# Raw weights fetched ahead, the first decay rows straight from SBUF: a change to the opening of a fused attention and two-MLP kernel

## The chip, the cores and the metric

The kernel runs on one core of a Trainium2 chip. The metric is the device time of one execution in microseconds (us); lower is better. Before the change it is 960.9 us, the median of 3 runs (960.6 to 962.42).

## What is computed

Three blocks follow one another: a causal attention with a decay, a layer that takes the maximum of three products, and a layer with a rational gate.

```python
scores = scale * np.matmul(q, k.transpose(0, 1, 3, 2))      # batch 4, 8 heads, 576 rows, width 64
cum = np.cumsum(np.log(np.clip(f, 0.0001, 1.0)), axis=-1)
scores = np.where(causal, -1e9, scores + cum[..., :, None] - cum[..., None, :])
attn = softmax(scores);  x = attn @ v                       # 2304 tokens of 512
h = np.maximum(np.maximum(x @ w1, x @ w2), x @ w3)          # 768 wide
x = h @ w_out
h = x @ w_in                                                # 2048 wide
out = (P(h) / (Q(h) + 1e-6)) @ w_out2
```

The weights arrive as 64-bit floats. They are fetched as pairs of 32-bit words, and the kernel itself makes 32-bit floats of them.

## The kernel before, in words

**Attention.** Work goes by pairs of heads; a pair holds two units, one for each head, for one group of query rows (320 or 256 of the 576). The first four pairs are those of the first batch with the group of 320. For a pair, `load` fetches the keys `kn` and queries `qn`, `load_v` the values; `prepare` transposes keys and queries on TensorE (tiles `tk`, `tq`), copies them into `kf` and `qf`, and in `copies` fetches two rows of the decay into `kf`. A unit then makes scores in three blocks of 64, 192 and 320 keys (`s`, L378), reduces them on VectorE (L382), takes exponentials on ScalarE (L388), normalises on GpSimd (L397), transposes back on TensorE (`tp`, L417), and, once both heads of a pair are there, multiplies by the values (`o`, L433). VectorE writes the result into `x` (L441). The lines are those of the kernel before.

**The decay.** `ncum` is the running sum of the logarithms, one scan over 576 columns for all 32 rows; `nch` holds it as a rounded part and a remainder. `nch` goes to `ncd` in DRAM, and every `kf` is filled from `ncd`.

**Fillers.** `exercised` puts `WARM` = 2 matmuls of 128x512 on a constant tile (`<-warm`, L84) ahead of the real work in each PSUM tile of the first four pairs. They compute nothing that is used.

**Weights.** Each of the 18 pieces of w1, w2, w3 goes through a conversion: `load_raw` (L165, 512 KB), a magnitude on ScalarE (`cv_w`, L179), four integer operations on VectorE (L184, L185, L186, L189), the rounded part on ScalarE (L195) and the remainder on GpSimd (L198). 12 smaller pieces of w_out follow. `pipelined` issues loads two conversions ahead (`LOOK`), and `conv_due` says at each fill how many conversions should be left.

**Order.** All loads are issued by SyncE (SP). Apart from the last stage, a scheduler with a model of time sets the order on each engine; `keep_in_program_order` holds single instructions in the order of the code. Each engine then runs its list strictly in order. The first product of the second block (`h`, L465) needs `x` of all four first pairs. From 74.45 us on TensorE works on that block between the units, and from 560 us on, at the latest, on the third block.

Of the kernel before, what the change touches and what calls it, by code (L numbers as in the profile page):

```python
# [8 lines left out]
F32 = mybir.dt.float32  # L9
F32R = mybir.dt.float32r  # L10
I32 = mybir.dt.int32
AF = mybir.ActivationFunctionType
ALU = mybir.AluOpType
# [11 lines left out]
GQ = [(0, 320), (320, 576)]  # L25
# [12 lines left out]
def kernel(  # L38
    ctx: ExitStack, tc: tile.TileContext, q, k, v, f, w1, w2, w3, w_out, m2_in, m2_out, m2_a, m2_b, out
):  # L40
    nc = tc.nc
    B, H, S, D = q.shape
# [3 lines left out]
    P = 128  # L46
# [6 lines left out]
    def r32(ap):  # L53
        return ap.bitcast(F32)

    def move(dst, src):
        return nc.sync.dma_start(r32(dst), r32(src))
# [7 lines left out]
    apool = apool_cm.enter_context(tc.tile_pool(name="apool", bufs=1, side="right"))  # L65
# [9 lines left out]
    warm = mpool.tile([P, 4, P], F32R, name="warm", tag="xo", bufs=2)  # L75
    for i in range(4):
        nc.vector.tensor_copy(warm[:, i], ident)
    wide = warm.rearrange("p i c -> p (i c)")

    def exercised(bank, n):  # L80

        if n < 4:
            for _ in range(WARM):
                nc.tensor.matmul(bank, warm[:, 0], wide, start=True, stop=True)  # L84
        return bank

    WARM = 2
# [13 lines left out]
    NR = B * H  # L101
    fl = apool.tile([NR, S], F32, name="fl", tag="vs", bufs=3)
    nc.sync.dma_start(fl, f.rearrange("b h s -> (b h) s"))
    ones = apool.tile([NR, S], F32, name="ones", tag="e4_0")
    nc.vector.memset(ones, 1.0)
    nc.vector.tensor_scalar(fl, fl, 1.0e-4, 1.0, op0=ALU.max, op1=ALU.min)
    nc.scalar.activation(fl, fl, AF.Ln)
    ncum = apool.tile([NR, S], F32, name="ncum", tag="vs", bufs=3)
    nc.vector.tensor_tensor_scan(ncum, ones, fl, 0.0, op0=ALU.mult, op1=ALU.subtract)
    nch = apool.tile([NR, 2, S], F32R, name="nch", tag="pt0")  # L110
    nc.vector.tensor_copy(nch[:, 0], ncum)
    nc.vector.tensor_tensor(nch[:, 1], ncum, r32(nch[:, 0]), op=ALU.subtract)
    ncd = dram.tile([NR, 2, S], F32R, name="ncd")
    move(ncd, nch)


    NKB, NQB = 4, (2, 3)
# [2 lines left out]
    LOOK, WHOLE, PRE = 2, 6, 2  # L120
# [123 lines left out]

        return [a, b, h, last]

    def pipelined(work, look):

        n = len(work)

        def go(i):
            for j in range(0 if i == 0 else i + look, min(i + look + 1, n)):
                work[j][0]()
            work[i][1]()

        return [lambda i=i: go(i) for i in range(n)]
# [5 lines left out]
    def pinned(ld):  # L262
        tc.keep_in_program_order(ld)
# [12 lines left out]
    class Pair:  # L276
# [58 lines left out]
        def copies(self):  # L335
            khi = GQ[self.groups[-1]][1]
            for h, i in enumerate(self.ik):
                k2 = kfs[i] if self.whole else k_split(i)[1]
                pinned(move(k2[D : D + 2, :khi], ncd[self.b * H + 2 * self.hp + h][:, :khi]))

        def prepare(self):
            return (
# [157 lines left out]
    def moe1_units(b, g):  # L500
        return [lambda fc=fc, j=j: moe1_h(b, g, fc, j) for fc in range(NF1) for j in range(3)] + [
            lambda dc=dc: moe1_o(b, g, dc) for dc in range(NDC)
        ]
# [14 lines left out]
        for fc in range(NF1)  # L518
        for z in range(2)
    ]  # L520
    conv = pipelined(conv, LOOK)
    wps = [(c, z) for c in range(NF2) for z in range(2)]
    conv2 = []
    for i, cz in enumerate(wps):
# [38 lines left out]
            state["of"] = max(1, NFILL * (ends[at] - step) - 3)  # L563
            state["n"], state["m"] = len(units), 0

    NCONV = len(conv)
    state["c"] = state["c2"] = 0.0

    def conv_due(step):
# [1 line left out]
        return NCONV - int(state["c"])  # L571

    pairs[0].load()
    pairs[0].load_v()
    LV = 1
    lvat = {}
    for p in pairs[1:]:
        lvat.setdefault(max(0, first[p.n] - LV), []).append(p)
    for f_ in pairs[0].prepare():
        f_()  # L580
    pairs[1].load()
    ab = const.tile([P, 8], F32, name="ab")
    pinned(nc.sync.dma_start(ab[:, 0:4], m2_a.partition_broadcast(P)))
    pinned(nc.sync.dma_start(ab[:, 4:6], m2_b.partition_broadcast(P)))
    for step in range(len(slots) + 2):
        u = slots[step] if step < len(slots) else None
        t = slots[step - 1] if 0 <= step - 1 < len(slots) else None
# [8 lines left out]
        if o:  # L596
            o.attend()
            if step in ready:
                queue.append((step, [x for bg in ready[step] for x in moe1_units(*bg)]))
        fill(step)  # L600
        if t:
            t.turn(0)
# [238 lines left out]
```

## Time and profile before

| what | value |
|---|---|
| median of 3 runs | 960.9 us |
| the profiled execution | 960.97 us |
| its span, first to last instruction | 959.2 us |
| TensorE busy | 935.4 us (98%) |
| VectorE busy | 729.2 us (76%) |
| ScalarE busy | 640.5 us (67%) |
| GpSimd busy | 253.6 us (26%) |
| granted TensorE clock, mean | 0.991 of full |

The profiled execution lies 0.07 us above the median, and 1.8 us of it lie outside the span. Busy time of TensorE counts the fillers too, so 98% isn't 98% of needed work. PE is TensorE's matmuls, DVE is VectorE, ACT ScalarE, POOL GpSimd; SPq is SyncE's list of transfers.

### The profile page before, as it was taken

Reading aid. Unit: us, or ns where it says so; the run is one execution under the profiler, and the core shown is the slowest. Engines: PE = TensorE matmul, PEld = TensorE weight load, DVE = VectorE, ACT = ScalarE, POOL = GpSimd, SP = SyncE. Lnnn points to the kernel's source line nnn. Section 1 sums busy time; section 2 is a strip of 40 time slices with the busy share of each in tenths; the row PEclk is TensorE's granted clock in tenths of the full one; section 3 lists DMA queues with packets and bytes.
Section 4 is the critical chain, followed back from the end, with each engine's and each line's share of the span. In section 5 each row is a group of like instructions: output and inputs, shape, how many; then the busy total and the mean of one; then the engine's idle time right before and its main releaser. Section 6 shows DMA issues by size and latency. Waiting matters only on the chain.

```text
span 959.2 us, 16834 instructions
## 1 busy us (share of the span) xinstructions
PE 935.4 (98%) x5780; PEld 827.2 (86%) x5780; DVE 729.2 (76%) x1689; ACT 640.5 (67%) x1526; POOL 253.6 (26%) x408
## 2 busy tenths in 40 slices
PE   8989899999999999999999999999999999999998
PEld 6758889997998989999999988888888888899997
DVE  5698985556676776634296969888988988899997
ACT  6886667777777676656444567667666666677765
POOL 2546654444554555424132400000000000000000
PEclk9978999999999999999999999999999999999999
DMA  6694323123456455220145477011002102100000
GB/s 164 167 247 138 84 68 85 43 76 86 131 152 193 139 168 145 86 90 1 58 139 179 144 252 275 1 44 44 1 1 66 44 1 66 45 1 1 33 1 33
DMA packets 125621, 88.52 MB, mean 92 GB/s; under 512 B 74448, under 2 KB 110304, under 8 KB 125536
## 3 DMA queue, kind: packets, MB, share of 16 engines
q1 hardware_dynamic: 125536, 87.45, 30.4%
q8 instruction: 46, 0.75, 0.3%
q14 instruction: 39, 0.32, 0.1%
HBM read 64.73 MB, written 22.69 MB: 91 GB/s over the span
## 4 chain that ended last, share of the span: by engine, by line
PE 76%; DVE 13%; ACT 4%; issue 3%; DMA 2%; SPq 1%; POOL 1%; ACTq 0%; POOLq 0%; DVEq 0%
PE hq L716 7%; PE hq L714 7%; PE oo L764 7%; PE oo L765 7%; PE hq L715 7%; PE oo L763 7%; PE h L465 5%; PE h L466 5%; PE h L467 5%; PE o L433 5%; PE tp L417 4%; PE s L380 2%; PE s L381 2%; PE x2p L491 2%; PE x2p L493 1%
## 5 line engine op out<-in xcount | busy, mean ns | idle before, releaser
L465 PE MATMUL h<-x,w1h 128*128 128x320 f32 (+1 forms) x576 | 176.2, 306 | 2.0 <-DVE x L441 1.1
L466 PE MATMUL h<-x,w1h 128*128 128x320 f32 (+1 forms) x576 | 172.7, 300 | 0.0
L467 PE MATMUL h<-x,w1l 128*128 128x320 f32 (+1 forms) x576 | 172.5, 300 | 0.0
L397 POOL TENSOR_SCALAR e<-e,rs 128x64 f32<-128x64 f32 (+4 forms) x160 | 88.8, 569 | 105.0 <-DVE rs L394 96.4
L388 ACT ACTIVATE e<-e,st 128x64 f32<-128x64 f32 (+4 forms) x160 | 89.1, 558 | 37.7 <-DVE st L382 36.7
L465 PEld LDWEIGHTS h<-x,w1h 128*128 128x128 f32 x576 | 109.9, 191 | 4.9 <-DVE x L441 2.0
L764 PE MATMUL oo<-wp,gh 128*128 128x512 f32 x288 | 112.6, 391 | 0.0
L763 PE MATMUL oo<-wp,gh 128*128 128x512 f32 x288 | 112.0, 389 | 0.0
L466 PEld LDWEIGHTS h<-x,w1h 128*128 128x128 f32 x576 | 110.0, 191 | 0.3 <-issue 0.2
L467 PEld LDWEIGHTS h<-x,w1l 128*128 128x128 f32 x576 | 109.9, 191 | 0.1
L723 ACT ACTIVATE s<-hq 128x512 f32<-128x512 f32 (+1 forms) x80 | 44.3, 554 | 98.0 <-PE hq L716 98.0
L765 PE MATMUL oo<-wp,gl 128*128 128x512 f32 x288 | 109.1, 391 | 0.0
L382 DVE CUSTOM_DVE_ANT_0 e<-s,mask 128x320 f32<-128x320 f32 (+3 forms) x160 | 67.8, 432 | 38.2 <-PE s L381 22.9
L419 ACT ACTIVATE pt<-tp 128x384 f32<-128x384 f32 (+3 forms) x160 | 69.8, 468 | 16.6 <-PE tp L417 13.8
L726 DVE SCALAR_TENSOR_TENSOR s<-s,ab,u 128x512 f32<-128x512 f32 (+1 forms) x80 | 55.7, 696 | 32.6 <-ACT u L724 32.4
L417 PE MATMUL tp<-ident,e 128*128 128x128 f32 (+1 forms) x480 | 77.4, 279 | 3.0 <-DVE k2s L310 1.7
L716 PE MATMUL hq<-x,wil 128*128 128x512 f32 (+1 forms) x192 | 69.8, 364 | 0.0
L714 PE MATMUL hq<-x,wih 128*128 128x512 f32 (+1 forms) x192 | 69.8, 363 | 0.0
L715 PE MATMUL hq<-x,wih 128*128 128x512 f32 (+1 forms) x192 | 69.6, 363 | 0.0
L765 PEld LDWEIGHTS oo<-wp,gl 128*128 128x128 f32 x288 | 54.0, 188 | 11.2
L763 PEld LDWEIGHTS oo<-wp,gh 128*128 128x128 f32 x288 | 54.1, 188 | 10.5
L764 PEld LDWEIGHTS oo<-wp,gh 128*128 128x128 f32 x288 | 54.0, 188 | 10.5
(131 smaller groups left out, 2429.4 us busy)
## 6 DMA issues: line engine op xcount, KB each, us to landing
raw_w<-in_moe_w_dram SPq DMA_DIRECT2D x18, 512.0 KB
raw_wp<-in_moe_w_out_dram SPq DMA_DIRECT2D x32, 256.0 KB
wpd<-wp SPq DMA_DIRECT2D x32, 256.0 KB
raw_wi<-in_moe_w_in_dram SPq DMA_DIRECT2D x32, 256.0 KB
wp<-wpd SPq DMA_DIRECT2D x10, 768.0 KB
x2d<-xo SPq DMA_DIRECT2D x16, 320.0 KB
out_dram<-ob SPq DMA_DIRECT2D x18, 256.0 KB
kn<-in_k_dram SPq DMA_DIRECT2D x32, 128.0 KB
```

What stands on the lines that cost most here:

```text
L388: nc.scalar.activation(e[:nr], e[:nr], AF.Exp, bias=m, scale=-1.0, accum_out=l)
L397: nc.gpsimd.tensor_scalar(e, e, self.rs[:, 1, j : j + 1], 0.0, op0=ALU.mult, op1=ALU.add)
L417: nc.tensor.transpose(tp[:kr, dst : dst + P], self.e[i][:, Q0[c] : Q1[c]], ident)
L465: nc.tensor.matmul(hp_[:, :w], wh[:, j, dc], xs[dc][:, 1], start=(dc == NDC - 1), stop=False)
L466: nc.tensor.matmul(hp_[:, :w], wh[:, j, dc], xs[dc][:, 0], start=False, stop=False)
L467: nc.tensor.matmul(hp_[:, :w], wl[:, j, dc], xs[dc][:, 0], start=False, stop=(dc == 0))
L714: nc.tensor.matmul(hp_[:, :w], wih[:, dc, fs], xh, start=(dc == 0), stop=False)
L715: nc.tensor.matmul(hp_[:, :w], wih[:, dc, fs], xl, start=False, stop=False)
L716: nc.tensor.matmul(hp_[:, :w], wil[:, dc, fs], xh, start=False, stop=(dc == NDC - 1))
L763: nc.tensor.matmul(o, g[0][:, ts_], wh_, start=(fc == 0), stop=False)
L764: nc.tensor.matmul(o, g[0][:, ts_], wl_, start=False, stop=False)
L765: nc.tensor.matmul(o, g[1][:, ts_], wh_, start=False, stop=(fc == NF2 - 1))
```

## The change

The scan runs in two stretches (320 and 256 columns), each split into its two parts at once. For the first pair the decay rows go from `nch` in SBUF straight into `kf`, a row at a time, in place of the way over `ncd`. The first three raw weights are fetched right behind the first pair's keys and queries; the first pair's values and the write of `ncd` come behind its `prepare`. Two conversions are put into the code ahead of the second pair's loads, with `NCONV` lowered by two, so that all later ones keep the same distance. The fillers of the first pair are held in program order. The two tiny loads of the third block's coefficients (`ab`) go to step 16.

```diff
             for _ in range(WARM):
-                nc.tensor.matmul(bank, warm[:, 0], wide, start=True, stop=True)
+                dense = nc.tensor.matmul(bank, warm[:, 0], wide, start=True, stop=True)
+                if n == 0:
+                    tc.keep_in_program_order(dense)
...
-    nc.vector.tensor_tensor_scan(ncum, ones, fl, 0.0, op0=ALU.mult, op1=ALU.subtract)
-    nch = apool.tile([NR, 2, S], F32R, name="nch", tag="pt0")
-    nc.vector.tensor_copy(nch[:, 0], ncum)
-    nc.vector.tensor_tensor(nch[:, 1], ncum, r32(nch[:, 0]), op=ALU.subtract)
+    for a, z in GQ:
+        part = slice(a, z)
+        sofar = ncum[:, a - 1 : a] if a else 0.0
+        nc.vector.tensor_tensor_scan(ncum[:, part], ones[:, part], fl[:, part], sofar, op0=ALU.mult, op1=ALU.subtract)
+        nc.vector.tensor_copy(nch[:, 0, part], ncum[:, part])
+        nc.vector.tensor_tensor(nch[:, 1, part], ncum[:, part], r32(nch[:, 0, part]), op=ALU.subtract)
     ncd = dram.tile([NR, 2, S], F32R, name="ncd")
-    move(ncd, nch)
...
-                pinned(move(k2[D : D + 2, :khi], ncd[self.b * H + 2 * self.hp + h][:, :khi]))
+                row = self.b * H + 2 * self.hp + h
+                if self.n == 0:
+                    for x in range(2):
+                        pinned(move(k2[D + x : D + x + 1, :khi], nch[row : row + 1, x, :khi]))
+                else:
+                    pinned(move(k2[D : D + 2, :khi], ncd[row][:, :khi]))
...
-    conv = pipelined(conv, LOOK)
+    ahead = [load_ for load_, _ in conv[: LOOK + 1]]
+    conv = pipelined(conv, LOOK, True)
...
-    NCONV = len(conv)
+    NCONV = len(conv) - 2
...
     pairs[0].load()
-    pairs[0].load_v()
+    for load_ in ahead:
+        load_()
...
     for f_ in pairs[0].prepare():
         f_()
+    move(ncd, nch)
+    pairs[0].load_v()
+    for _ in range(2):
+        conv.pop(0)()
     pairs[1].load()
     ab = const.tile([P, 8], F32, name="ab")
-    pinned(nc.sync.dma_start(ab[:, 0:4], m2_a.partition_broadcast(P)))
-    pinned(nc.sync.dma_start(ab[:, 4:6], m2_b.partition_broadcast(P)))
```

In the lists below the number at a name's end is a running one; the second `kn` and the second `tk` are the second pair's. Line numbers of the changed kernel are higher: L165 is L169 there, L267 and L270 are L271 and L274, L332 is L336, L378 is L387, L417 is L426.

SP's list of transfers before, from the end of the first pair's queries on:

```order
L267 DMA v_140<-in_v_dram 128x2x64
L270 DMA v_140<-in_v_dram 128x2x64 x2
L267 DMA v_285<-in_v_dram 128x2x64
L267 DMA kn_163<-in_k_dram 128x2x64
L57 DMA ncd<-nch 32x1152
L270 DMA kn_163<-in_k_dram 128x2x64 x2
L270 DMA v_285<-in_v_dram 128x2x64
L57 DMA kf_114<-ncd 2x320
L57 DMA kf_115<-ncd 2x320
```

The same place of SP's list in the changed kernel:

```order
L169 DMA raw_w_0_142<-in_moe_w_dram 128x4x256
L169 DMA raw_w_0_144<-in_moe_w_dram 128x4x256
L169 DMA raw_w_0_146<-in_moe_w_dram 128x4x256
L57 DMA kf_116<-nch 1x16x20 x2
L57 DMA kf_117<-nch 1x16x20 x2
L57 DMA ncd<-nch 32x1152
L271 DMA v_169<-in_v_dram 128x2x64
L274 DMA v_169<-in_v_dram 128x2x64 x2
L169 DMA raw_w_1_183<-in_moe_w_dram 128x4x256
L271 DMA kn_194<-in_k_dram 128x2x64
L274 DMA kn_194<-in_k_dram 128x2x64 x2
```

Three raw weights now stand ahead of the first pair's decay rows, and a fourth ahead of the second pair's keys, which stood fourth in the piece before and now stand behind twelve other transfers.

TensorE's list before, from the first pair's first filler on (`s_0_0_0_0` are the scores of its first head, `tp_0_0_0` that head's transposes):

```order
L84 MATMUL s_0_0_0_0_186<-warm 128x512 x2
L84 MATMUL s_0_0_0_0_193<-warm 128x512 x2
L84 MATMUL o_1_0_367<-warm 128x512 x2
L332 MATMUL tq_0_154<-ident,qn_132 128x128 x3
L84 MATMUL tq_0_206<-warm 128x512 x2
L332 MATMUL tk_0_173<-ident,kn_163 128x128 x3
L378 MATMUL s_0_0_0_0_186<-kf_114,qf_118 128x64
L378 MATMUL s_0_0_0_0_193<-kf_114,qf_118 128x192
L84 MATMUL tp_0_0_0_243<-warm 128x512 x2
L84 MATMUL s_0_0_0_0_200<-warm 128x512 x2
L378 MATMUL s_0_0_0_0_200<-kf_114,qf_118 128x320
```

And in the changed kernel, from the second pair's transposes on:

```order
L336 MATMUL tk_0_202<-ident,kn_194 128x128 x3
L84 MATMUL s_0_0_0_0_215<-warm 128x512 x2
L387 MATMUL s_0_0_0_0_215<-kf_116,qf_120 128x64
L84 MATMUL s_0_0_0_0_222<-warm 128x512 x2
L387 MATMUL s_0_0_0_0_222<-kf_116,qf_120 128x192
L336 MATMUL tq_0_235<-ident,qn_193 128x128 x3
L84 MATMUL tp_0_0_0_266<-warm 128x512 x2
L84 MATMUL s_0_0_0_0_229<-warm 128x512 x2
L387 MATMUL s_0_0_0_0_229<-kf_116,qf_120 128x320
L426 MATMUL tp_0_0_0_266<-ident,e_0_0_0_221 128x128
L426 MATMUL tp_0_0_0_266<-ident,e_0_0_0_228 128x128 x2
```

The second pair's transposes of its keys stand ahead of the first scores in both. The fillers of `s` and `o`, six matmuls, moved from ahead of the first transposes of queries to behind them, and the first head's transposes `tp` now stand ahead of the second head's scores, which before ran first.

## Rows read from the trace of the kernel before

**Rows 1.** The page, busy time, share of the span and instructions.

```profile
PE 935.4 (98%) x5780; PEld 827.2 (86%) x5780; DVE 729.2 (76%) x1689; ACT 640.5 (67%) x1526; POOL 253.6 (26%) x408
```

**Rows 2.** Stretches: us, busy PE PEld DVE ACT POOL, clock, DMA share, GB/s.

```profile
10.52:27.84 17.32, 17.14 (x97) 13.39 (x98) 9.26 (x37) 14.59 (x46) 7.53 (x11) 1.00 0.71 188
27.84:50.20 22.36, 22.36 (x133) 17.48 (x132) 13.99 (x46) 18.60 (x57) 11.00 (x18) 1.00 0.63 167
50.20:73.90 23.70, 19.94 (x80) 11.97 (x78) 23.48 (x49) 19.16 (x47) 11.73 (x13) 0.75 0.89 246
79.30:133.76 54.46, 51.33 (x363) 46.26 (x361) 49.52 (x113) 34.09 (x86) 33.03 (x40) 1.00 0.33 88
133.76:142.00 8.24, 6.24 (x39) 5.02 (x39) 5.64 (x16) 6.00 (x17) 6.84 (x11) 1.00 0.19 60
```

**Rows 3.** The line of time, TensorE: start, us, instruction, idle before.

```profile
4.23 1.22 PE L84 MATMUL tk<-warm 128*128 128x512 f32 x2 [4.23 <-DVE warm L77]
...
7.60 1.11 PE L84 MATMUL s<-warm 128*128 128x512 f32 x4
...
9.81 0.71 PE L332 MATMUL tk<-ident,kn 128*128 128x128 f32 x3
10.52 0.79 PE L378 MATMUL s<-kf,qf 66*128 66x64 f32 x4
...
12.08 0.70 PE L378 MATMUL s<-kf,qf 66*128 66x320 f32 x2
...
25.57 1.41 PE L433 MATMUL o<-pt,v 128*64 128x320 f32 x12
```

**Rows 4.** The line of time, SP's issues of transfers.

```profile
4.21 0.47 SPq L267 DMA_DIRECT2D v<-in_v_dram  x1
...
6.31 0.41 SPq L267 DMA_DIRECT2D kn<-in_k_dram  x1
7.02 0.33 SPq L57 DMA_DIRECT2D ncd<-nch  x1
...
9.12 0.59 SPq L57 DMA_DIRECT2D kf<-ncd  x2
...
15.95 1.57 SPq L165 DMA_DIRECT2D raw_w<-in_moe_w_dram  x3
```

**Rows 5.** Waits of SP's list, first 50 us: total, times, longest.

```profile
SPq L270 <- DMA raw_w<-in_moe_w_dram: 1.9, 2, 1.0
SPq L267 <- DMA raw_w<-in_moe_w_dram: 1.3, 1, 1.3
```

**Rows 6.** The line of time, ScalarE.

```profile
11.35 0.35 ACT L388 ACTIVATE e<-e,st 128x64 f32<-128x64 f32 x1
...
19.86 0.67 ACT L179 ACTIVATE cv_w<-raw_w 128x512 f32<-128x512 f32 x1 [0.18 <-DMA raw_w<-in_moe_w_dram]
...
21.43 0.68 ACT L179 ACTIVATE cv_w<-raw_w 128x512 f32<-128x512 f32 x1 [0.35 <-DMA raw_w<-in_moe_w_dram]
```

**Rows 7.** The line of time, VectorE, the decay's scan and remainder.

```profile
4.38 1.35 DVE L109 TENSOR_TENSOR_SCAN ncum<-ones,fl 32x576 f32<-32x576 f32 x1 [0.21 <-ACT fl L107]
...
6.24 0.75 DVE L112 TENSOR_TENSOR nch<-ncum,nch 32x576 fp32r<-32x576 f32 x1
```

**Rows 8.** The line of time, GpSimd, the first unit's normalisation.

```profile
14.73 1.22 POOL L397 TENSOR_SCALAR e<-e,rs 128x64 f32<-128x64 f32 x3 [4.91 <-DVE rs L394]
```

**Rows 9.** VectorE busy on tile cv_w alone, by stretch, with clock and DMA.

```profile
27.84:50.20 22.36, 8.77 (x16) 1.00 0.63 167
50.20:73.90 23.70, 18.67 (x24) 0.75 0.89 246
```

**Rows 10.** TensorE by stretch: us, busy, clock, DMA share, GB/s.

```profile
62.24:74.45 12.21, 9.64 (x29) 0.50 0.62 172
74.45:79.30 4.85, 4.85 (x18) 0.50 0.66 218
```

**Rows 11.** The fillers (L84) alone: us, busy PE and PEld, clock, DMA.

```profile
10.52:74.45 63.93, 31.25 (x90) 14.76 (x90) 0.90 0.74 201
```

More of the change, by code (lines that the diff above doesn't have):

```diff
@@ L105 @@
     nc.vector.memset(ones, 1.0)
+    ncum = apool.tile([NR, S], F32, name="ncum", tag="vs", bufs=3)
+    nch = apool.tile([NR, 2, S], F32R, name="nch", tag="pt0")
     nc.vector.tensor_scalar(fl, fl, 1.0e-4, 1.0, op0=ALU.max, op1=ALU.min)
     nc.scalar.activation(fl, fl, AF.Ln)
-    ncum = apool.tile([NR, S], F32, name="ncum", tag="vs", bufs=3)
-    nc.vector.tensor_tensor_scan(ncum, ones, fl, 0.0, op0=ALU.mult, op1=ALU.subtract)
-    nch = apool.tile([NR, 2, S], F32R, name="nch", tag="pt0")
-    nc.vector.tensor_copy(nch[:, 0], ncum)
-    nc.vector.tensor_tensor(nch[:, 1], ncum, r32(nch[:, 0]), op=ALU.subtract)
+    for a, z in GQ:
[4 more added lines that the diff above has]
+        nc.vector.tensor_tensor(nch[:, 1, part], ncum[:, part], r32(nch[:, 0, part]), op=ALU.subtract)
     ncd = dram.tile([NR, 2, S], F32R, name="ncd")
-    move(ncd, nch)
     NKB, NQB = 4, (2, 3)
@@ L245, in stages_wp, with pipelined @@
         return [a, b, h, last]
-    def pipelined(work, look):
+    def pipelined(work, look, begun=False):
         n = len(work)
         def go(i):
-            for j in range(0 if i == 0 else i + look, min(i + look + 1, n)):
+            for j in range(0 if i == 0 and not begun else i + look + (i == 0), min(i + look + 1, n)):
                 work[j][0]()
@@ L599 @@
                 queue.append((step, [x for bg in ready[step] for x in moe1_units(*bg)]))
+        if step == 16:
+            pinned(nc.sync.dma_start(ab[:, 0:4], m2_a.partition_broadcast(P)))
+            pinned(nc.sync.dma_start(ab[:, 4:6], m2_b.partition_broadcast(P)))
         fill(step)
```

## The prediction

> **What bounds the kernel now.** The page's busy row comes first: TensorE is at work in 935.4 of 959.2 us [rows 1], so 24 us of its idle time, and what its clock loses, are all that can be won. The stretches say where these lie. From 10.52 to 50.20 us TensorE is busy in 39.5 of 39.7 us at the full clock, while VectorE is busy in 9.26 and 13.99 us only [rows 2]. It is busy because of the fillers: they alone take 31.25 us between 10.52 and 74.45 us [rows 11]. An engine that runs its list in order and has no gap there catches nothing up, so whatever delays the first scores at 10.52 us delays the first four pairs by as much. From 50.20 to 73.90 us the bound is VectorE (23.48 of 23.70 us), and 18.67 us of that are 24 operations on `cv_w`, six conversions at 3.11 us. Earlier, 16 operations took 8.77 us, 2.19 us a conversion [rows 2, 9]. TensorE's clock is at half, 1.2 GHz, from 62.24 to 79.30 us [rows 10]. VectorE stays near its limit until 133.76 us (49.52 of 54.46), and TensorE loses 3.13 us in that stretch and 2.00 us in the next one [rows 2].
>
> **The change part by part.** *Decay.* Before, the chain is scan, cast, remainder from 4.38 to 6.99 us [rows 7], then `ncd` is written at 7.02 and `kf` filled from it at 9.12 us [rows 4]. For 320 of 576 columns the first stretch's three operations are 320/576 of 2.61 us, 1.45 us; the second scan, which stands ahead of the first remainder, adds 256/576 of 1.35, 0.60 us. The rows are ready at 6.4 us in place of 7.0, and the way over DRAM, 2.1 us, is gone: `kf` could be asked for 2.7 us sooner.
>
> *Raw weights.* They take from that. Three of them go out where the values' loads went, from 4.21 us on, and the decay rows come behind them in the same list. Before, three raw weights were issued within 1.57 us from 15.95 on [rows 4]; the first one's conversion began at 19.86, the second's at 21.43 us, each right after waiting for its transfer [rows 6]. So one lands 3.9 us after its issue and the next ones 1.57 us apart: they pass one after another. By this the three land at 8.1, 9.7 and 11.3 us, and the decay rows behind them not before 11.3. The Trainium skill's page "DMA: Bandwidth & Descriptors", section "Two DMAs through the same engine are not ordered", says that within one queue of a DMA engine descriptors start in order; the spacing of 1.57 us agrees, and by the page too the small transfer gets no way past the large ones.
>
> *The second pair's keys.* In the list TensorE must transpose them ahead of the first scores, before and after. Before they were issued from 6.31 us on and transposed at 9.81 us [rows 3, 4]. Now the write of `ncd`, three loads of values and a fourth raw weight stand ahead of them. Loads of values and of keys, which read nothing of the weights, already wait for raw weights to land, 1.9 and 1.3 us [rows 5]: SP issues no transfer until the eighth ahead of it is done (the program gives its transfers eight semaphores in turn). Counting back by eight, the three loads of values wait for the three raw weights (8.1, 9.7, 11.3 us), the fourth raw weight and the keys for the decay rows. So that weight goes out at 11.4 and lands at 15.3 us, and the keys, issued from 11.9 to 13.4 us and passing behind it, are there at about 16.0 us. Three transposes (0.71 us) and two fillers (half of 1.11 us) later the first scores start, at 17.2 in place of 10.52 us: **+6.7 us** [rows 3]. Bounds: if SP did not wait, keys issued at 10.4 us and behind the fourth weight would be there at 13.4, +4.2 us; if the fourth weight takes the 4.9 us that the second of the three did from its issue, +7.7 us.
>
> *Conversions.* In VectorE's list four of them now stand ahead of the first reduction: 4 x 2.19 = 8.8 us, which from 8.8 us on end at 17.6 us, about when the first scores are there. They hide behind the wait above and cost nothing more; without it they would hold the first exponential, at 11.35 us before [rows 6], until then. Up to the third `x` there are eight conversions in the list in place of six, between the first and the fourth `x` as many as before. So the stretches from 27.84 to 73.90 us keep their lengths, and two conversions fewer are left behind, 2 x 3.11 = 6.2 us of VectorE [rows 9].
>
> *The order on TensorE.* The first head's `tp` now stands ahead of the second head's scores. From the end of the last scores, 12.78 us, to the end of the normalisation, 15.95 us, it was 3.2 us [rows 3, 8]; TensorE has a pair of fillers to put into that (0.55 us) and waits for the rest, **+2.5 us** (bounds 1.5, if two of the three normalised blocks are enough to go on, and 3.2). The six moved fillers took 1.4 us of a time before the first scores; one pair is in the sum above, the others, **+0.9 us**, now come behind (bounds 0 and 1.4).
>
> *The rest.* The `ab` loads go to a stretch in which transfers are scarce (DMA share 0.33 and 0.19 from 79.30 us on [rows 2]), hidden, and their removal from SP's early list saves nothing, since SP waits for landings there. Holding the fillers in order changes nothing by itself beyond the places shown.
>
> *Sum.* The first product of values, at 25.57 us before [rows 3], comes 6.7 + 2.5 + 0.9 = 10.1 us later, and so do the stretches up to the fourth `x`. Given back is what TensorE loses from 79.30 to 142 us, 5.1 us at most, since VectorE has 6.2 us less to do there; I take 4, as part of these gaps waits for other engines. 10.1 - 4 = +6.1 us. Against the profiled execution's 960.97 us, which is 0.07 us above the median of the runs, that makes **967.0 us**.
>
> **The rivals.**
> *VectorE decides, and the early work is free: faster.* VectorE's work up to 133.76 us is the same in both kernels, and in the first 50 us it sat idle for 8.1 + 8.4 us between 10.52 and 50.20 alone [rows 2]. If the second pair's keys came as early as before and the fillers left gaps to catch up, the two conversions' 6.2 us would be won less some delay: 960.97 - 6.2 + 1 to 4, about 957 us. It decides where the front's delay is below what is given back, 5 us. Against it stand the 39.5 busy us of 39.7 on TensorE. Chance 0.18.
> *Front and give-back cancel.* A delay of 5 us (the lower bound of the keys and a short bubble) and 5.1 us back: 961 us, within 0.2% (1.9 us), which is about what a measurement of this kernel can tell from no change. Chance 0.10.
> *The clock falls in the new wait: slower still.* TensorE would be idle from about 9 to 16 us. In rows 10 the clock was at half after gaps that VectorE had made, and came back 4.85 us after dense work began at 74.45 us; at the start two fillers took 1.22 us against half of 1.11 us later [rows 3]. If it falls, the first 5 us or more of work behind the wait run at half speed: 2.5 us, and with the bubble in between 5 us more. With little given back, 967 + 5 to 8, about 973 us. The Trainium skill's page "TensorE: Matmul & The Clock Gate", section "What's actually happening", says that the throttled state is the default and activity releases it; the trace agrees with a clock that falls at 62.24 us. Chance 0.17.
> *My forecast*, a delay of 9 to 13 us of which 3 to 5 come back: 964 to 971 us. Chance 0.55.
>
> **How the numbers follow.** Slower by over 0.2%: 0.55 + 0.17 = 0.72; same 0.10; faster 0.18. The forecast's own range is 964 to 971 us. For 8 in 10 the range takes in the upper half of the faster case, no change, and most of the fallen clock: 958.5 to 974 us. The lists also differ in places up to some 360 us, where the model of time shifts things; I put that at 2 us either way, the size of the gap in the last stretch of rows 2, an estimate that lies inside.
>
> **What would show it.** In the changed kernel's trace: the decay rows' and keys' transfers waiting for raw weights in SP's list, the first scores at 17 us and the first product of values at 35 to 36 us; a gap on TensorE of some 7 us before the second pair's transposes and one of 2.5 us before the second head's scores; the first `h` at about 84 us, with 14 conversions done, not 12; less idle time of TensorE between then and the eighth unit pair. It is wrong if first scores come before 13 us, or if TensorE shows gaps among the fillers that take the delay up.

## The result and the profile after

The changed kernel takes **968.84 us** (median of 4 runs, 968.62 to 970.98) against 960.75 us of the kernel before beside it (960.0 to 962.42): ratio 1.0084, interval 1.0073 to 1.0096, 8.1 us slower. The profiled execution spans 967.1 us, that of before 959.2.

The page's busy row of the changed kernel, to be read against [rows 1]: TensorE is busy longer by 2.8 us, though its instructions are the same 5780.

```profile
PE 938.2 (97%) x5780; PEld 829.3 (86%) x5780; DVE 726.6 (75%) x1692; ACT 643.1 (66%) x1526; POOL 250.9 (26%) x408
```

The line of time of SP's issues in the changed kernel, beside [rows 4]: three raw weights, then four small rows of `kf`, `ncd`, the values, a fourth raw weight, and only then the second pair's keys, at 12.24 in place of 6.31 us.

```profile
4.22 1.57 SPq L169 DMA_DIRECT2D raw_w<-in_moe_w_dram  x3
5.91 2.49 SPq L57 DMA_DIRECT2D kf<-nch  x4
8.50 0.52 SPq L57 DMA_DIRECT2D ncd<-nch  x1
...
11.67 0.47 SPq L169 DMA_DIRECT2D raw_w<-in_moe_w_dram  x1
12.24 0.45 SPq L271 DMA_DIRECT2D kn<-in_k_dram  x1
```

TensorE's line of time in the changed kernel, beside [rows 3]. The first two score blocks now start at 18.75, not 10.52 us; ahead of them is a wait of 7.85 us for the second pair's keys, behind them one of 2.63 us for the first head's normalised `e`; the first product of values starts at 39.87, not 25.57 us.

```profile
16.86 1.23 PE L336 MATMUL tk<-ident,kn 128*128 128x128 f32 x3 [7.85 <-DMA kn<-in_k_dram]
17.75 1.20 PE L84 MATMUL s<-warm 128*128 128x512 f32 x2
18.75 0.52 PE L387 MATMUL s<-kf,qf 66*128 66x64 f32 x2
...
25.98 1.20 PE L426 MATMUL tp<-ident,e 128*128 128x128 f32 x3 [2.63 <-POOL e L406]
...
39.87 1.41 PE L442 MATMUL o<-pt,v 128*64 128x320 f32 x12
```

TensorE by stretch in the changed kernel (us, busy, granted clock, DMA share, GB/s). These three are at half clock. The third answers to [rows 10]; the first two are new, one after each wait.

```profile
11.96:22.20 10.24, 5.24 (x17) 0.50 0.57 141
25.62:29.03 3.41, 3.02 (x10) 0.50 0.73 245
76.82:93.88 17.06, 14.46 (x50) 0.50 0.54 159
```

To see where the delay goes, `x` is the best milepost: ScalarE copies each product of values once, 32 times (L440 before, L449 after). Its 1st, 3rd, 4th, 9th and last, first in the kernel before, then in the changed one:

```profile
27.36 0.44 ACT L440 ACTIVATE x<-o 128x320 fp32r<-128x320 f32 x1
...
49.73 0.44 ACT L440 ACTIVATE x<-o 128x320 fp32r<-128x320 f32 x1
...
71.86 0.43 ACT L440 ACTIVATE x<-o 128x320 fp32r<-128x320 f32 x1
...
161.81 0.44 ACT L440 ACTIVATE x<-o 128x320 fp32r<-128x320 f32 x1
...
479.19 0.39 ACT L440 ACTIVATE x<-o 128x256 fp32r<-128x256 f32 x1 [4.91 <-PE o L433]
```

```profile
41.62 0.44 ACT L449 ACTIVATE x<-o 128x320 fp32r<-128x320 f32 x1
...
64.46 0.44 ACT L449 ACTIVATE x<-o 128x320 fp32r<-128x320 f32 x1
...
86.52 0.43 ACT L449 ACTIVATE x<-o 128x320 fp32r<-128x320 f32 x1
...
169.44 0.44 ACT L449 ACTIVATE x<-o 128x320 fp32r<-128x320 f32 x1
...
487.24 0.39 ACT L449 ACTIVATE x<-o 128x256 fp32r<-128x256 f32 x1 [4.91 <-PE o L442]
```

The shift is 14.3 us at the first `x`, 14.7 at the third and the fourth, 7.6 at the ninth and 8.05 at the last, which is the span's difference of 7.9. So the delay arises before the first `x`, goes on whole to the fourth, and half of it comes back between the fourth and the ninth. What VectorE spends on `cv_w` there is, before and then after (us, busy, count, clock, DMA share, GB/s):

```profile
71.90:161.80 89.90, 19.35 (x25) 0.96 0.34 94
```

```profile
86.50:169.40 82.90, 12.70 (x18) 0.96 0.32 86
```

6.65 us less conversion in the stretch, and the stretch is 7.0 us shorter. The two numbers are close, but the first doesn't explain the second. All engines in the same stretch, before and then after (us, busy PE PEld DVE ACT POOL, clock, DMA share, GB/s):

```profile
71.90:161.80 89.90, 83.14 (x575) 74.15 (x575) 72.70 (x182) 59.88 (x159) 51.47 (x70) 0.96 0.34 94
```

```profile
86.50:169.40 82.90, 78.91 (x550) 70.28 (x550) 64.29 (x169) 56.18 (x151) 45.26 (x65) 0.96 0.32 86
```

VectorE is idle for a fifth of it in both kernels. TensorE is the busier engine: it runs 25 matmuls of `h` fewer there, which in the changed kernel stand behind the ninth `x` (4.2 us less work), and it is idle for 4.0 us in place of 6.8.

TensorE's own balance says where the 7.9 us are. Up to the first `x`, and from the ninth to the last, before and then after (us, busy, clock, DMA share, GB/s):

```profile
0.00:27.36 27.36, 22.93 (x117) 1.00 0.63 161
161.81:479.19 317.38, 313.57 (x2471) 1.00 0.36 105
```

```profile
0.00:41.62 41.62, 26.78 (x114) 0.84 0.48 133
169.44:487.24 317.80, 316.33 (x2497) 1.00 0.36 104
```

Up to the first `x` TensorE is idle for 14.8 us in place of 4.4, 10.4 more; from the fourth to the last `x` it is idle for 5.5 us in place of 10.6, 5.1 less. Over the whole span its idle time is 5.1 us longer. Its work in stretches at half clock is 22.72 us in place of 14.49 [rows 10], and half of the difference, 4.1 us, is what that costs. The sum is 9.2 us. The 1.3 us by which the same matmuls take less elsewhere stay open.

### The profile page after: what moved, and what is told of

Its sections match the earlier page's. It is cut to its first block, busy times and chain, and to the rows that moved or that the text cites. A ratio compares the mean times of both kernels' runs of the same rounds, so it can differ in the third digit from the quotient of the medians.

```text
span 967.1 us, 16828 instructions
## 1 busy us (share of the span) xinstructions
PE 938.2 (97%) x5780; PEld 829.3 (86%) x5780; DVE 726.6 (75%) x1692; ACT 643.1 (66%) x1526; POOL 250.9 (26%) x408
## 4 chain that ended last, share of the span: by engine, by line
PE 82%; DVE 8%; ACT 3%; DMA 2%; issue 2%; POOL 2%; SPq 1%; POOLq 0%; ACTq 0%; DVEq 0%
PE hq L732 7%; PE hq L730 7%; PE oo L781 7%; PE oo L780 7%; PE hq L731 7%; PE oo L779 7%; PE h L474 6%; PE h L475 6%; PE h L476 6%; PE o L442 5%; PE tp L426 5%; PE s L389 2%; PE x2p L500 2%; PE x2p L502 2%; PE s L390 2%
## 5 line engine op out<-in xcount | busy, mean ns | idle before, releaser
L391 DVE CUSTOM_DVE_ANT_0 e<-s,mask 128x320 f32<-128x320 f32 (+3 forms) x160 | 67.5, 432 | 46.1 <-PE s L390 26.8
L428 ACT ACTIVATE pt<-tp 128x384 f32<-128x384 f32 (+3 forms) x160 | 70.5, 470 | 22.4 <-PE tp L426 20.8
L426 PE MATMUL tp<-ident,e 128*128 128x128 f32 (+1 forms) x480 | 79.0, 281 | 3.4 <-POOL e L406 2.9
L426 PEld LDWEIGHTS tp<-ident,e 128*128 128x128 f32 (+1 forms) x480 | 56.4, 134 | 10.3 <-POOL e L406 4.7
L781 PEld LDWEIGHTS oo<-wp,gl 128*128 128x128 f32 x288 | 54.0, 188 | 11.4
L780 PEld LDWEIGHTS oo<-wp,gh 128*128 128x128 f32 x288 | 54.0, 188 | 10.5
```

Of the source, the lines that this page charges most:

```text
L426: nc.tensor.transpose(tp[:kr, dst : dst + P], self.e[i][:, Q0[c] : Q1[c]], ident)
L780: nc.tensor.matmul(o, g[0][:, ts_], wl_, start=False, stop=False)
L781: nc.tensor.matmul(o, g[1][:, ts_], wh_, start=False, stop=(fc == NF2 - 1))
```

## The experiments

Two theories stood at the start. The prediction's: the raw weights ahead of the second pair's keys make the front late, and the hold on the fillers adds only the bubble. Its rival: the hold makes the loss by itself. The first four runs told these apart. "Theory" in their expectations is the first, and "rival A" of e1 and e2 is the second; e3 and e5 have rivals of their own.

**e1: the raw weights and conversions back in their old places**; direct decay rows, hold and the new place of `ab` stay.

```diff
-    ahead = [load_ for load_, _ in conv[: LOOK + 1]]
-    conv = pipelined(conv, LOOK, True)
+    conv = pipelined(conv, LOOK)
...
-    for load_ in ahead:
-        load_()
...
-    for _ in range(2):
-        conv.pop(0)()
```

> The changed kernel with raw weights and conversions back in their old places; the decay in two stretches, its direct way for the first pair and the held fillers stay. Theory (the raw weights ahead of the second pair's keys make TensorE's wait, the held fillers only add the bubble): the keys land near 11 us, first scores near 12 in place of 18.75 us, the bubble of 2.6 us before the second head's scores stays, the first product of values comes 4 to 5 us later than before and nothing is given back: 963 to 966 us. Rival A (the held fillers make the loss by themselves): 967 us or more. Rival B (the early conversions are all of it): 961 us.

971.68 us, ratio 1.0104 (1.0089 to 1.0119): slower than the whole change. The theory missed, the rival held. TensorE still waits for the second pair's keys (2.59 and 0.92 us) and for `e` (2.71 us), its clock is at half from 11.50 to 18.33 and 21.74 to 25.15 us, and the first `x` is at 38.7 us. Without any raw weight in front, the first `x` is late by 11.3 us.

**e5: the whole change without the hold.**

```diff
-                dense = nc.tensor.matmul(bank, warm[:, 0], wide, start=True, stop=True)
-                if n == 0:
-                    tc.keep_in_program_order(dense)
+                nc.tensor.matmul(bank, warm[:, 0], wide, start=True, stop=True)
```

> The changed kernel with the first pair's fillers no longer held in order. In TensorE's list the first scores now stand ahead of the second pair's transposes, and the second head's scores ahead of the first head's transposes back. Theory (raw weights cost only because the first scores stand behind the second pair's keys): first scores near 12 us, behind the decay rows' landing, no bubble, the first product of values 2 to 5 us later than before, 4 to 6 us given back: 957 to 961 us. Rival A (three raw weights and four conversions ahead hold the start whatever TensorE's order): first scores or first exponential near 18 to 20 us, 965 to 969 us.

959.95 us, ratio 0.9984 (0.9974 to 0.9994), in the theory's range. TensorE's line of time in this kernel shows what the hold had decided: with the fillers free, the first scores stand ahead of the second pair's transposes. The keys are as late as in the changed kernel (16.53 us), but the scores, at 11.92 us, wait only for their decay rows.

```profile
11.92 0.79 PE L385 MATMUL s<-kf,qf 66*128 66x64 f32 x4 [1.73 <-DMA kf<-nch]
...
16.53 0.33 PE L334 MATMUL tk<-ident,kn 128*128 128x128 f32 x1 [1.72 <-DMA kn<-in_k_dram]
```

**e3: the kernel before with the decay edits alone** (two stretches, `kf` of the first pair straight from `nch`, `ncd` written behind its `prepare`).

```diff
+    for a, z in GQ:
+        part = slice(a, z)
...
+                if self.n == 0:
+                    for x in range(2):
+                        pinned(move(k2[D + x : D + x + 1, :khi], nch[row : row + 1, x, :khi]))
```

> The kernel before with the decay in two stretches and its direct way for the first pair alone. Theory: the decay rows are asked for near 6.5 us and land near 8.5 us, the first scores start 1 to 2 us earlier than 10.52 us, and since TensorE is then filled by fillers without a gap, the whole kernel ends 1 to 2 us earlier: 959 to 960 us. Rival (first scores wait for the queries' copy, not for the decay rows): 961 us, within 0.2%.

958.19 us, ratio 0.9962 (0.9949 to 0.9975), faster than both ranges. The first scores come at 10.20 us, 0.3 us earlier than before in place of 1 to 2, and the first `x` is no earlier (28.0 us). The gain stands elsewhere: from the third to the fourth `x` it takes 18.7 us, not 22.1. In that stretch VectorE's list has 7 of the following units' reductions where it had 10. And TensorE works 8.38 us at half clock (62.64 to 76.29 us) in place of 14.49; half of the difference is 3.05 us, as much as the span's gain of 3.1. Whether the order of the reductions is the reason was not tested.

**e2: the changed kernel with the second pair's loads ahead of the raw weights.** The raw weights move with that behind the first pair's decay rows and the write of `ncd`.

```diff
-    for load_ in ahead:
-        load_()
...
     move(ncd, nch)
+    pairs[1].load()
+    for load_ in ahead:
+        load_()
...
-    pairs[1].load()
```

> The changed kernel with the second pair's loads ahead of the raw weights in the code; the fillers are held, two conversions at once stay. Theory (the wait is that of the second pair's keys): first scores near 12 us, a bubble before the second head's scores that now holds the four conversions (raw weights issued near 11 land from 15 us on, the fourth conversion ends near 22 us), the first product of values 5 to 9 us later than before, 4 to 6 us given back: 961 to 965 us. Rival A (the held fillers make the loss by themselves): 967 us or more.

970.34 us, ratio 1.0087 (1.0072 to 1.0102). The keys come earlier and the first scores start at 13.13 us in place of 18.75, yet the first `x` is at 41.7 us: the wait has only moved to `e`. TensorE's row, then GpSimd's and two of VectorE's in e2:

```profile
24.67 0.47 PE L426 MATMUL tp<-ident,e 128*128 128x128 f32 x1 [7.04 <-POOL e L406]
```

```profile
21.21 1.33 POOL L202 TENSOR_TENSOR w1l<-cv_w,w1h 128x512 fp32r<-128x512 f32 x1 [9.52 <-ACT w1h L199]
22.53 3.28 POOL L406 TENSOR_SCALAR e<-e,rs 128x64 f32<-128x64 f32 x3
```

```profile
17.08 0.43 DVE L188 TENSOR_SCALAR cv_w<-cv_w 128x512 f32<-128x512 f32 x1 [1.43 <-ACT cv_w L183]
...
18.61 0.48 DVE L391 CUSTOM_DVE_ANT_0 e<-s,mask 128x320 f32<-128x320 f32 x1
```

The conversions, which in the changed kernel hide behind the wait for keys, stand in three engines' lists ahead of the first head's softmax; and the hold has put that head's `tp` ahead of everything else that TensorE could do.

The new theory after these four: the hold fixes an order on TensorE in which each early wait is met at full length; early conversions give back some 6 us later, whatever the front does.

**e8: the kernel before with the hold alone.**

```diff
-                nc.tensor.matmul(bank, warm[:, 0], wide, start=True, stop=True)
+                dense = nc.tensor.matmul(bank, warm[:, 0], wide, start=True, stop=True)
+                if n == 0:
+                    tc.keep_in_program_order(dense)
```

> The kernel before with one thing added: the fillers of the first pair are held in the order in which they are written. Decay, raw weights, conversions and ab stay as before. New theory (holding is what costs: the first head's tp is put ahead of the second head's scores, the fillers that stood in the waits come later, TensorE's clock falls in the gaps, and the front's delay is carried to the end unshortened): the first product of values some 6 to 9 us later than the 25.57 us of before, time 966 to 971 us. Theory of the prediction (holding costs only the places named there, 2.5 + 0.9 us, and the raw weights the rest): 963 to 965 us. Third possibility (holding does nothing without the direct decay rows): 960 to 962.5 us.

969.15 us, ratio 1.0072 (1.0056 to 1.0088): the new theory's range. The keys cost 1.09 us here, the bubble before `tp` is 2.49 us, and the clock is at half behind it; its row and the stretch:

```profile
16.76 1.20 PE L419 MATMUL tp<-ident,e 128*128 128x128 f32 x3 [2.49 <-POOL e L399]
```

```profile
16.15:22.97 6.82, 6.18 (x19) 0.50 1.03 305
```

6.18 us of work at half clock are 3.1 us lost. First `x` 35.3 us, 7.9 us late, and the last one is 8.5 us late.

**e9 and e13: which fillers.** e9 holds those on the score banks alone, e13 all others of the first pair.

```diff
-    def exercised(bank, n):
+    def exercised(bank, n, held=False):
...
-                if n == 0:
+                if held and n == 0:
...
-                sp = exercised(ps_s.tile([P, 512], F32, name=f"s{i}_{n}_{self.nm}", tag="s"), p.n)
+                sp = exercised(ps_s.tile([P, 512], F32, name=f"s{i}_{n}_{self.nm}", tag="s"), p.n, True)
```

(e13: the default is `True`, and the score banks pass `False`.)

> The kernel after, but of the first pair's fillers only those on the score banks s are held; those on tk, tq, tp and o are free. In the order of this kernel the second pair's three key transposes and the first head's tp stand where they stand in after, ahead of the first scores and of the second head's scores. New theory (the place of these rows is the cost, and the fillers on s are what fixes it): first scores at 17 to 19 us, time 966 to 970 us. Rival (it is the number of held fillers, or the hold on tp and o, that costs): 959 to 963 us.

> The kernel after, with all fillers of the first pair held except those on the score banks s: the other half of e9. In its order the first scores stand ahead of the second pair's transposes again, but the fourth x stands behind the scores of the next unit on VectorE, as in after and unlike e9 and e5. New theory (two separate prices of the hold: the fillers on s set the front, the others set the place of the fourth x): first product of values at 30 to 32 us, third to fourth x 21 to 23 us in place of 18 to 20, time 962 to 965 us. Rival 1 (only the fillers on s cost): 959 to 961 us. Rival 2 (any hold costs the whole): 967 to 970 us.

e9 took 963.15 us, ratio 1.0015 (1.0004 to 1.0026), 2.9 us below the theory's range and 0.15 above the rival's: by its time the theory missed. Its front is that of the changed kernel (first scores 18.99, first `x` 42.1 us), so the fillers on the score banks set the front, as the theory had it. But its fourth `x` follows the third after 17.7 us, as in e3 and e5, where the changed kernel needs 22.1. Against no hold at all (e5), this half of the hold makes the first `x` 9.7 us later and the time 3.2 us longer.

e13 took 970.96 us, ratio 1.0085 (1.0069 to 1.0100), 1 us above the range of rival 2, though not by its mechanism: first scores 11.98, first product of values 31.9, third to fourth `x` 23.4 us, as the new theory had it to within 0.4 us, and the ninth `x` stands at 162.8 us, 1.0 us after that of before. It then loses 11.4 us between there and the last `x`, where no other kernel loses over 1.4. Two places of it are at half clock, with TensorE busy throughout (its stretches, as above):

```profile
295.77:299.18 3.41, 3.41 (x16) 0.50 0.58 199
357.21:364.03 6.82, 6.78 (x27) 0.50 0.35 100
```

They explain 5.1 us. Another 5.8 are work: 50 matmuls more fall between the ninth and the last `x`, 32 of them of `x2p`, which before run behind the last `x`. TensorE's idle time there is only 0.5 us longer. What puts the clock at half in those places, and so much work there, stays open. The two halves of the hold cost 3.2 and 11.0 us against e5, and both together 8.9 us: the price doesn't divide between them.

**e6: fillers into the wait for the keys**, to keep the clock up there.

```diff
     WARM = 2
+    EXTRA = 30
...
+            if self.n == 1 and which == "k" and g == 0:
+                for _ in range(EXTRA):
+                    tc.keep_in_program_order(nc.tensor.matmul(t, warm[:, 0], wide, start=True, stop=True))
```

> The kernel after, with 30 more fillers (some 7 us of TensorE at the full clock) on the bank tk of the second pair, ahead of its three transposes; they change no result. They fill the wait for the second pair's keys. If TensorE's clock at half after that wait is a part of the front's delay: the clock stays at full speed from 8.5 us to the second gap, the 5.3 us of work between 16.86 and 22.20 us take half as long, and 2 to 3 us are saved, 965.5 to 967.5 us. If the clock costs nothing there, because what follows waits for VectorE anyway: 968 to 970 us, and more if the fillers overrun the keys' landing.

972.94 us, ratio 1.0113 (1.0099 to 1.0127), above both ranges. The clock does stay up, the first scores start 1.2 us earlier (17.53 us), but at the second wait only 1.0 us of that is left, and behind it the clock falls for longer than in the changed kernel, 24.28 to 31.11 us against 25.62 to 29.03:

```profile
24.95 1.20 PE L430 MATMUL tp<-ident,e 128*128 128x128 f32 x3 [2.81 <-POOL e L410]
```

```profile
7.22:24.28 17.06, 12.33 (x57) 1.00 0.78 214
24.28:31.11 6.83, 6.12 (x19) 0.50 0.33 94
```

First `x` 42.0 us, none the earlier. What follows waits for VectorE, as the second half of the expectation had it: TensorE now waits 1.37 us for the first head's reductions. VectorE makes these from 20.59 us on, right behind its conversions, and in the changed kernel from 20.79 us on. So these fillers could not buy off the clock behind the first wait. The span is 4.2 us longer than the changed kernel's. The loss lies behind the front: 2.2 us between the fourth and the ninth `x`, where 17 more matmuls fall into the stretch, and 2.4 behind the last `x`, where the clock is at half from 563.59 to 567.00 us. What moved these stays open.

**e4: the raw weights and two early conversions alone**, on the kernel before.

```diff
+    ahead = [load_ for load_, _ in conv[: LOOK + 1]]
+    conv = pipelined(conv, LOOK, True)
...
+    for load_ in ahead:
+        load_()
...
+    pairs[0].load_v()
+    for _ in range(2):
+        conv.pop(0)()
```

> The kernel before with the middle part of the change alone: three raw weights loaded ahead of the values and of the second pair's loads, two conversions at once. Decay rows by way of DRAM as before, fillers free, ab at its old place. In this kernel's order the second pair's transposes stand ahead of the first scores, as in before. Theory of the prediction for this part (+6.7 us at the first scores, carried on, and a give-back of some 4 us): first scores at 17 us or later, time 963 to 966 us. New theory (same delay in front, but two early conversions give back 6 to 7 us, and the fourth x comes earlier in VectorE's list than in before, which e3 and e5 showed to be worth 3 to 4 us): first scores at 17 to 20 us, time 958 to 962 us. Rival (raw weights ahead of the keys cost nothing): first scores before 13 us, time 952 to 956 us.

964.18 us, ratio 1.0023 (1.0013 to 1.0032). That is in the range of the prediction's theory, and 2 us above the new theory's. In this list the transposes do stand ahead of the first scores, and the scores are late by about what the prediction worked out:

```profile
14.89 1.24 PE L332 MATMUL tk<-ident,kn 128*128 128x128 f32 x3 [2.44 <-DMA kn<-in_k_dram]
15.93 0.85 PE L332 MATMUL tq<-ident,qn 128*128 128x128 f32 x3
16.57 1.28 PE L378 MATMUL s<-kf,qf 66*128 66x64 f32 x4
```

First scores 6.05 us late against the predicted 6.7, 0.4 us ahead of what both theories have; first `x` 9.1 us late, and by the ninth `x` all but 0.5 us is back: 5.4 of it between the fourth and the ninth, 3.3 between the third and the fourth. The last `x` is 1.9 us late.

**e10, e12 and e11: no hold, second pair's loads first**, with two, no and four early conversions (e10 is e2 without the hold; the others change `range(2)` and `NCONV`).

```diff
-    for _ in range(2):
+    for _ in range(4):
         conv.pop(0)()
```

> The kernel after without the hold, and with the second pair's loads ahead of the raw weights and the first pair's values: direct decay rows and two conversions early, both without what the new theory holds for their price. New theory (the front's delay is carried to the end whole, and two early conversions give back 6 to 7 us between the first and the ninth x, or 3 to 4 us beside the direct decay rows): the first product of values at 26 to 29 us, time 953 to 957 us, ahead of the 958.2 us of decay alone. Rival (early conversions only win back what they delayed themselves; with a front as early as before there is nothing to win): 958 to 960.5 us.

> The kernel of e10 (no hold, second pair's loads first, then the raw weights), but no conversion is done ahead of its time: the raw weights lie loaded and wait. New theory (the gain of e10 over decay alone is VectorE's: two conversions done in idle time are two fewer in the stretch that VectorE bounds): fourth to ninth x back at 90 us or more, time 958 to 961 us. Rival (the gain comes from the loads, which are out of the way later): 954 to 956.5 us.

> The kernel of e10 with four conversions at once in place of two (six raw weights loaded ahead of the third pair's keys). If VectorE still bounds the stretch from the fourth to the ninth x and the idle time in front holds two more conversions: 3 to 6 us less than e10, 949 to 952 us. Rival (six raw weights at 1.57 us each now hold up the third pair's keys, which TensorE transposes at 22 us in e10, and the conversions hold up the first units' reductions; the fourth x stands late again): first product of values later than 29 us, time 954 to 959 us.

e10 took **954.91 us**, ratio 0.9929 (0.9916 to 0.9942), the fastest of all kernels here and 15.4 us faster than e2, from which it differs by the hold alone; e12 958.44 (ratio 0.9956, 0.9942 to 0.9970). Both stand where the new theory put them. VectorE's time on `cv_w` between the fourth and the ninth `x`, e10 and then e12:

```profile
72.20:154.90 82.70, 15.43 (x20) 0.96 0.36 98
```

```profile
69.00:160.80 91.80, 21.43 (x30) 0.95 0.37 101
```

6.0 us less conversion, a stretch shorter by 9.1 us, and 3.8 us of it left at the last `x`. The fronts agree (first `x` 29.4 and 28.9 us), so two conversions done early are worth 3.5 us in the time. The 9.1 us are more than that give-back: e12 runs 21 matmuls more in the stretch, and its clock falls there a second time (us, busy, clock, DMA share, GB/s):

```profile
133.47:140.29 6.82, 6.28 (x25) 0.50 0.49 144
```

Over the whole span, 4.3 us shorter in e10, TensorE is idle for 2.6 us less and does 2.9 us less work at half clock, 1.5 us less of loss. e11 took 964.3 us, ratio 1.0025 (1.0016 to 1.0033): two more conversions overfill the front. Its first product of values, at 27.9 us, isn't late as the rival had it, and the first `x` is still at 30.5 us, but the second comes at 50.2, against 43.1 in e10, behind conversions, and the clock is at half from 23.34 to 30.17 us. The rival's side, by more than its range.

All runs beside one another (us). First scores come from TensorE's line of time and `x` from ScalarE's. Idle is TensorE's idle time in the span, half its busy time in stretches at half clock. All these are of the profiled execution, which lies within 1 us of the median, but for e9 (2.3 us above) and e13 (1.8 above). The time is the median. The kernel of before took 961.9 to 962.3 us beside the experiments, and each ratio above is against the runs beside it.

| kernel | first scores | 1st x | 3rd to 4th x | 4th to 9th x | last x | idle | half | time |
|---|---|---|---|---|---|---|---|---|
| before | 10.5 | 27.4 | 22.1 | 89.9 | 479.2 | 23.8 | 14.5 | 960.75 |
| after | 18.8 | 41.6 | 22.1 | 82.9 | 487.2 | 28.9 | 22.7 | 968.84 |
| e3 decay alone | 10.2 | 28.0 | 18.7 | 91.1 | 476.0 | 25.0 | 8.4 | 958.19 |
| e8 hold alone | 11.4 | 35.3 | 23.2 | 91.3 | 487.7 | 29.2 | 20.8 | 969.15 |
| e4 raw and conversions alone | 16.6 | 36.5 | 18.8 | 84.6 | 481.1 | 24.7 | 16.3 | 964.18 |
| e1 without raw and conversions | 14.0 | 38.7 | 22.3 | 90.1 | 490.3 | 31.5 | 19.1 | 971.68 |
| e5 without hold | 11.9 | 32.5 | 18.9 | 86.1 | 477.7 | 24.0 | 11.9 | 959.95 |
| e2 keys first | 13.1 | 41.7 | 21.6 | 84.9 | 488.4 | 31.6 | 21.4 | 970.34 |
| e10 keys first, no hold | 11.1 | 29.4 | 19.8 | 82.7 | 473.1 | 19.2 | 10.1 | 954.91 |
| e12 as e10, none early | 9.8 | 28.9 | 17.9 | 91.8 | 476.9 | 21.8 | 13.0 | 958.44 |
| e11 as e10, four early | 11.0 | 30.5 | 21.6 | 85.1 | 481.2 | 25.9 | 12.5 | 964.30 |
| e9 hold on score banks | 19.0 | 42.1 | 17.7 | 84.9 | 483.4 | 27.2 | 16.3 | 963.15 |
| e13 hold on the rest | 12.0 | 33.3 | 23.4 | 83.4 | 491.6 | 26.8 | 32.4 | 970.96 |
| e6 more fillers | 17.5 | 42.0 | 21.8 | 85.1 | 489.1 | 28.5 | 20.8 | 972.94 |

The spans follow the last two columns: idle time and half of the work at half clock account for each kernel's difference from before to within 1.6 us, but for e6, whose 30 more fillers are work of their own.

## Why the prediction was right in its time and wrong in one cause

The sum, +6.1 us, came out as +7.9 in the span. That it came so near is partly luck, since two terms were too small by amounts that mostly cancel. Point by point:

*The delay is carried: right.* From the first to the fourth `x` the two kernels take 44.5 and 44.9 us. From the first to the last `x` e8 and e1 keep theirs too (7.9 and 8.5 us; 11.3 and 11.1 us); e9 doesn't (14.8 and 4.2 us).

*Transfers: right.* Conversions begin as the raw weights land, in ScalarE's line of time after:

```profile
8.32 0.67 ACT L183 ACTIVATE cv_w<-raw_w 128x512 f32<-128x512 f32 x1 [1.31 <-DMA raw_w<-in_moe_w_dram]
...
9.81 0.68 ACT L183 ACTIVATE cv_w<-raw_w 128x512 f32<-128x512 f32 x1
11.27 0.67 ACT L183 ACTIVATE cv_w<-raw_w 128x512 f32<-128x512 f32 x1 [0.78 <-DMA raw_w<-in_moe_w_dram]
```

Forecast were 8.1, 9.7 and 11.3 us. The first and the third of these began after waiting for their transfers; the second only shows that its weight had landed. The decay rows behind them arrive by 11.92 us (e5), against "not before 11.3"; without raw weights ahead of them the scores start at 10.20 (e3). The Trainium skill's page "DMA: Bandwidth & Descriptors", section "Two DMAs through the same engine are not ordered", says that descriptors in one queue of an engine start in order; these rows agree, since the small rows get no way past. The keys were due at 16.0 and are transposed at 16.86 us.

*First scores, +6.7 us: +8.2.* Of the 1.5 us, 0.9 are the keys; the rest is the clock, at which three transposes and two fillers take 16.86 to 18.75 us, 1.9 us, where 1.3 were counted.

*Bubble, +2.5 us: 2.63.* Right.

*Moved fillers, +0.9 us: +3.5.* This is the mis-sized term: 14.3 - 8.2 - 2.63. Little of it is fillers: from the first scores to the first product of values TensorE runs 34 of them before and 36 after, some 0.5 us more. What the term left out is the rival "the clock falls in the new wait", which happened. In that stretch 6.5 us of work stand at half clock, 3.2 us of loss; with the work just ahead of it, whose 0.6 us of loss are in the term above, it is at most 4.1 us (half of 5.24 and of 3.02). The Trainium skill's page "TensorE: Matmul & The Clock Gate", section "What's actually happening", has the throttled state as the default that activity releases; the trace agrees, with the clock up from 8.55 us after work that began at 4.23, and down from 11.96 us after idling from 9.0. But in e6, with the clock kept up behind the first wait, nothing was won: VectorE's conversions were the next bound.

*Conversions hide behind the wait: right, but narrowly, and so was what they would do without it* (e2, a bubble of 7.04 us). They were to be done at 17.6 us; VectorE is done with them, and begins its reductions, at 20.79 us, 1.5 us after the first scores are there, and TensorE doesn't have to wait for it.

*Give-back, 4 us with a ceiling of 5.1: 6.6 by the last `x`.* The place was right: TensorE's idle time between the fourth and the last `x` falls by 5.1 us, the ceiling itself. Of TensorE's waits between the fourth and the ninth `x`, VectorE ended 5.2 us before and 3.0 us in the changed kernel. The other 1.5 us stand in TensorE's busy time and aren't explained. That VectorE's 6.65 us came back whole, as the faster rival has it, isn't shown, since the 7.0 us between the fourth and the ninth `x` hold 4.2 us of TensorE's work that comes later. e10 against e12 shows the same kind of gain: 2.6 us less idle time, and less time at half clock. The rival failed all the same, since 6.6 is less than the front's 14.7. The two errors, +4.6 at the fourth `x` and +2.6 in what comes back, mostly cancel.

*First `h` at 84 us: wrong.* It is at 93.2 us, 6.7 us behind the fourth `x` (before 2.6), since the fifth product now stands ahead of it.

*The step that failed:* "Holding the fillers in order changes nothing by itself beyond the places shown." The late keys were put down to the raw weights, because the transposes stood ahead of the first scores both before and after. But the raw weights make the keys late, and with the decay rows coming directly it is the hold that makes the scores wait for them: without it the first scores stand ahead of the transposes (e3, e5). With the decay by way of DRAM the transposes stand ahead in the free order too (before, e4). With the raw weights and without the hold the loss is gone (e5, -0.16%); with the hold and without the raw weights it is larger than with both (e1, +1.04%); and the hold alone makes most of it (e8, +0.72%). In e8 the keys cost only 0.9 us at the first scores; most of the rest of its front is the bubble before `tp` and the clock behind it. e9 and e13 show that the fillers on the score banks set the front; which of the held fillers make the loss in time they don't show. The raw weights' own price at the first scores, with the transposes ahead, is near the forecast (e4, 6.05 us), and by the ninth `x` all but 0.5 us is back.

*Decay, worth 2.7 us in the readiness of `kf`: not worth it there* (0.3 us at the first scores); e3's gain of 0.38% stands in less work at half clock about the fourth `x`. The time from the third to the fourth `x` doesn't simply go with the hold: it is 22.1 us in the kernel before, which has none, and 17.7 in e9. What in the scheduler decides it was not tested.

## What to carry to other kernels

Ask of an order constraint what the free order had used the constrained instructions for: these fillers had stood in the waits, and pinning them moved real work behind a transfer. Check a reason that rests on two edits at once by taking each away. Work moved into an idle front pays only up to what the front holds: against none, two early conversions gave 3.5 us and four cost 5.9. And a stretch between two mileposts can grow shorter because work moved across the milepost, so read the busiest engine's idle time, and its time at half clock, before giving a reason.

## What was not expected of the hardware

Keeping TensorE busy through the first wait halved the time at half clock ahead of the first `x`, 13.65 us in the changed kernel and 6.83 in e6, and the first `x` came 0.4 us later. And in e13 the clock fell at 357.21 us though TensorE had been busy for 2.93 of the 4.21 us before, its gaps 0.6 us at the longest.
